# An attention and expert kernel: second pass's first chunk on one batch, two-operand work off GpSimd, the first bias tile in halves

## The chip, the cores and the metric

The kernel runs on one core of one Trainium2 chip. The metric is device time in microseconds, from runs on the chip; one further execution was taken with the hardware profiler. All times below are from these.

## The reference

Three layers follow each other. The first is attention with a bias that a small network computes from the distance of two positions; the second gives every token the weighted sum of four experts; the third multiplies two projections element by element and projects the product.

```python
# B, H, S, D = 2, 8, 576, 64; 1152 tokens of 512; 4 experts of 1024; last layer 1536 wide
scores = q @ k.T / sqrt(D)
x = log1p(abs(i - j)) / log1p(max(i, 1))
scores += (relu(x[..., None] @ w1 + b1) @ w2).transpose(2, 0, 1)
attn = softmax(scores);  x = (attn @ v) as tokens by H * D
p = probs / probs.sum(-1)
x = sum(p[:, e] * (relu(x @ moe_w1[e]) @ moe_w2[e]) for e in range(4))
out = ((x @ w_a) * (x @ w_b)) @ w_out
```

## The kernel before

**A planner writes the program.** Every piece of work is an `op` with the engines that may do it and an estimated cost on each, the tiles it reads and writes, and a rank. `Plan.run` goes through estimated time and gives each free engine the waiting piece of lowest rank that can start; the order so found is each engine's program. On the chip the engines then work through their programs in order and wait for each other by semaphores. A cost, an engine list or a dependency that changes therefore reorders everything behind it. `ENGINES` says which engines may do which kind of piece, `RELUS` how many of a bias group's four lookups ScalarE does. Pools of tiles are `Room`s: a piece starts only when there is a free place for its result, and places are handed out in the order of asking.

**Attention.** The bias is made in 36 groups of 16 rows (`bias_group`): four lookups `hh`, each a maximum against a shifted table on VectorE (L365) or a relu on ScalarE (L367), then four products on TensorE (`pb`, L379), an output `bst` (ScalarE L397 or VectorE L399), a mirror copy of its other side (L236, the shared helper for copies), and a store to DRAM (`bias_d`, L410). A bias tile `bt` for 128 rows and two heads is read back with shifted rows (L466). The first eight groups (rank `bias0`) serve the first 128 rows.

For each pair of heads `m` and batch `b`, rows 0 to 127 come first, then rows 128 to 575 in two parts. Scores `ps` (L516 in plain float32 for the first rows, later L498 with the queries split in a high part `qh` and a rest `ql`, L451), the sum with the bias and the row minimum in one VectorE instruction (L501), the exponential on ScalarE (L511), transposes to `ptb` (L533), one over the row sums (L573, L574, tiles `sums`, `rx`, `rb`), the product with the values `pv` (L598), and the result in two parts, `x_hi` and `x_lo` (L607).

**Experts.** All products are of split operands, high times high, high times low and low times high. A weight unit is loaded to a staging tile `wst` (L639), cast to `wh` (L640) and the rest `wl` is taken (L641). `w1_item` makes the up-products `up` (L730) of one chunk of tokens, one expert and a quarter of its width, and the hidden tile `hh`, `hl` (L757, L758); `w2_item` makes the down-products `pz` (L741) and adds them to `acc`. The tokens are ordered so that the first 128 of both batches are columns 0 to 255, then come 448 of batch 0, then 448 of batch 1. Pass 0 takes chunk 0 (columns 0 to 255) and needs the first attention rows only, so it runs as filler, at a late rank, beside the rest of the attention. Pass 1 takes, for each expert, chunk 1 (columns 256 to 639) and chunk 2 (columns 640 to 1151).

Beside pass 1 the last layer's weights, which come as float64, are taken apart in words on VectorE (`convert`, L658 to L679); for `w_out` one subtraction (L678) may run on GpSimd. Behind the passes a Strassen-like product (`ab_item`, L864) and the last projection follow.

**Places.** Split weights have two places from the start, one in `mid`, one more when the values are done, three in `late` when the bias is done (`bias_end`) and one when attention is done (`attn_end`). The hidden tiles of pass 1 (`h2`) get two places when attention is done.

Of the kernel before, what the change touches and what calls it, by code (L numbers as in the profile page):

```python
# [9 lines left out]
F32 = mybir.dt.float32  # L10
# [9 lines left out]
P = 128  # L20
# [18 lines left out]


RANK = {"prep": 0.5, "bias0": 0, "bias1": 0.6, "bias2": 1, "split": 1, "load": 2, "chain": 0, "fill": 2, "x64": 3, "evac": -0.5, "fin": 0, "pv": 0, "split2": 1.5, "px": 0, "evac2": -0.5, "h2": 0}
ENGINES = {"kcast": "ACT DVE", "ksub": "POOL DVE", "qcast": "DVE", "qsub": "POOL DVE", "pt": "ACT DVE", "tail": "ACT DVE", "side": "ACT DVE", "mirror": "POOL ACT",
           "whi": "ACT DVE", "wlo": "DVE", "xhi": "DVE", "xlo": "POOL DVE", "rb": "ACT DVE", "rx": "ACT DVE", "s64": "POOL DVE",
           "wsum": "POOL DVE", "whi2": "ACT", "wlo2": "DVE", "px": "ACT DVE", "xsum": "DVE", "xhi2": "ACT", "xlo2": "DVE", "hmul": "DVE", "hlo": "DVE"}
QUICK, BY_AGE, MARGIN, LEAD = 0.9, True, 300, 2

# [44 lines left out]
class Plan:  # L91
# [9 lines left out]
    def op(self, eng, fn, r=(), w=(), rw=(), hold=(), prio=0, lock=False, after=(), size=0):  # L101

        o = Op()
        o.eng, o.fn, o.prio, o.lock, o.size = eng, fn, prio, lock, size
        o.after, o.n, o.done = [], len(self.ops), False
        deps = set(after)
        for b in r:
            deps.update(b.writers)
        for b in rw:
            deps.update(b.writers)  # L110
            deps.update(b.readers)
        for b in rw:
# [12 lines left out]
        self.ops.append(o)
        return o
# [102 lines left out]
def tile_kernel(ctx, tc, qd, kd, kf, vd, cst, probs, w1r, w2r, war, wbr, wor, out):  # L229
# [21 lines left out]
    def tp(stack, name, **kw):  # L251
        return stack.enter_context(tc.tile_pool(name=name, bufs=1, reuse_waits="tile", **kw))

    def place(room, pool, tag, n, shape, dt=F32, mark=None, pair=False):
        for i in range(n):
            def make(name, i=i):
                if pair:
                    return tuple(pool.tile(shape, dt, tag=f"{tag}{i}{z}", name=f"{name}{z}", bufs=1) for z in "hl")
                return pool.tile(shape, dt, tag=f"{tag}{i}", name=name, bufs=1)
            room.add(make, 1, mark)  # L260
# [13 lines left out]
    hp = tp(hp_stack, "hp", side="right")  # L274


    R = {z: Room() for z in "w wst h1 h2 u z p q2 q k2 k kq v bt ptb pr rb xf sums rx hh bst ct sum s64 t64 hl64".split()}
    R["s"], R["tv"] = Room(False), Room(False)
    ps_a = tp(attn, "ps_a", space=PSUM)
    ps_b = tp(solo, "ps_b", space=PSUM, side="right")  # L280
# [39 lines left out]
    NG = S // 4  # L320
    cs_t = hp.tile([P, S + NG + NU + 2 + 32], F32, name="cs")
    cs, pos = Buf(t=cs_t), hp.tile([P, NU, max(RELUS.values())], F32, name="pos")
    corr = {n: hp.tile([P, 1], F32, name=f"corr{n}") for n in sorted(set(RELUS.values()))}
    tab, neg_ = cs_t[:, 0:S], cs_t[:, S:S + NG]
    rinv, cw, w2s = cs_t[:, S + NG:S + NG + NU], cs_t[:, S + NG + NU:S + NG + NU + 2], cs_t[:, S + NG + NU + 2:]
    op({"SP": 440}, lambda e: nc.sync.dma_start(out=cs_t, in_=cst), w=[cs], size=P * 3160)
# [27 lines left out]
    rows, early = [], []  # L354

    def bias_group(u, rank):
        pri, acts = RANK[rank], RELUS[rank]
        before, after, n = dist(u)
        hs = []
        for g in range(4):  # L360
            G = 4 * u + g
            hh = new("hh")
            hs.append(hh)
            if g < 4 - acts:
                op({"DVE": n / 1.92 + 130}, lambda e, hh=hh, G=G: nc.vector.tensor_scalar(out=hh.t[:, :n], in0=tab[:, :n], scalar1=neg_[:, G:G + 1], scalar2=None, op0=ALU.max), r=[cs], w=[hh], prio=pri, lock=True)  # L365
            else:
                op({"ACT": n / 1.2 + 220}, lambda e, hh=hh, G=G: nc.scalar.activation(out=hh.t[:, :n], in_=tab[:, :n], func=AF.Relu, bias=pos[:, u, g - 4:][:, :1]), r=[cs], w=[hh], prio=pri)  # L367
        pb = new("tv" if n <= 512 else "s", "pb")
        bst = new("bst")


        def base():
            return (pb.t, 0) if n <= 512 else (pb.t.rearrange("p a b -> p (a b)"), 512 - n // 2)

        def mm(e):
            t, o = base()
            for lo, hi in ((0, n),) if n <= 512 else ((0, n // 2), (n // 2, n)):
                for g in range(4):
                    nc.tensor.matmul(t[32 * g:32 * g + 32, o + lo:o + hi], w2s, hs[g].t[:, lo:hi], start=True, stop=True)  # L379

        op({"PE": n * 1.67 + 170}, mm, r=[*hs, cs], w=[pb], hold=[bst], prio=pri)


        def ends():
            t, o = base()
            b = bst.t
            if before >= after:
                side = b[:, 0:before + 1], t[:, o:o + 1 + before][:, ::-1]
                rest = b[:, before + 1:before + after], b[:, before - after + 1:before][:, ::-1]
            else:  # L390
                side = b[:, before:before + after], t[:, o:o + after]
                rest = b[:, 0:before], b[:, before + 1:2 * before + 1][:, ::-1]
            return side, rest

        def put(e, out, src):
            if e == "ACT":
                nc.scalar.activation(out=out, in_=src, func=AF.Identity, scale=rinv[:, u:u + 1], bias=corr[acts])  # L397
            else:
                nc.vector.tensor_scalar(out=out, in0=src, scalar1=rinv[:, u:u + 1], scalar2=corr[acts], op0=ALU.mult, op1=ALU.add)  # L399

        def mirror(e):
            copy(e, *ends()[1])

        m = min(before, after - 1)
        side = op({e: v + 95 for e, v in t_psum(n, ENGINES["side"]).items()}, lambda e: put(e, *ends()[0]), r=[pb, cr], w=[bst], prio=pri)
        op({e: v for e, v in {"POOL": 2 * m + 150, "ACT": m / 1.2 + 95, "DVE": m / 0.96 + 68}.items() if e in ENGINES["mirror"].split()}, mirror, w=[bst], after=[side], prio=pri)
        rows.append(Buf(t=bias_d))

        def store(e):
            nc.sync.dma_start(out=bias_d[16 * u:16 * u + 16, :, S - before:S + after].rearrange("i h j -> (i h) j"), in_=bst.t[:, :before + after])  # L410

        o = op({"SP": 440}, store, r=[bst], w=[rows[u]], prio=pri, size=P * 4 * (before + after))
        if u == P // 16 - 1:
            early.append(o)
# [41 lines left out]
    def bias_tile(m, t):  # L456
        for x in bias_seq[-3:]:
            if x[:2] == (m, t):
                return x[2]
        bt = new("bt")  # L460
        bias_seq.append((m, t, bt))

        def load(e):
            b = bt.t
            if t < 4:
                nc.sync.dma_start(out=b, in_=bias_rows(t * P, P, 2 * m, 2))  # L466
            else:
                nc.sync.dma_start(out=b[0:D, 0:1], in_=bias_rows(4 * P, D, 2 * m, 1))
                rest = bias_rows(4 * P, D, 2 * m + 1, 1)
                nc.sync.dma_start(out=b[D:P, 0:1, :S - D], in_=rest[:, :, D:])  # L470
                nc.sync.dma_start(out=b[D:P, 0:1, S - D:], in_=rest[:, :, :D])

        need = min(P * t + P, S) // 16
        op({"SP": 440 if t < 4 else 1320}, load, r=rows[:need], w=[bt], size=P * 8 * S)
        return bt

    def step(m, b, t, k, q0, Q, qw, K, ptb, sums):
# [233 lines left out]
    late = {}  # L711
# [34 lines left out]
    def w1_item(p, e, c, q):  # L746
        t0, nt = CHUNKS[c]
        n = nt * P
        h = new("h1" if p == 0 else "h2", "h")
        if (p, e, q, 0) not in WU:  # L750
            WU[p, e, q, 0] = unit(w1r[e, q])
        xs = [X[b, p] for b in range(B)]
        for ft in range(2):
            u, last = up(WU[p, e, q, 0], ft, t0 * P, n, xs, [h])
            for t in range(t0, t0 + nt):
                ups.setdefault(t, []).append(last)
            relu = op({"ACT": n / 1.2 + 68}, lambda en, ft=ft, u=u: nc.scalar.activation(out=h.t[0][:, ft, :n], in_=u.t[:, :n], func=AF.Relu), r=[u], w=[h])  # L757
            op({"DVE": n / 0.96 + 68}, lambda en, ft=ft, u=u: nc.vector.scalar_tensor_tensor(out=h.t[1][:, ft, :n], in0=u.t[:, :n], scalar=0.0, in1=f(h.t[0][:, ft, :n]), op0=ALU.max, op1=ALU.subtract), r=[u], w=[h], after=[relu])  # L758
        return h
# [300 lines left out]

    def bias_end():
        hp_stack.close()
        place(R["w"], tp(ctx, "late", side="right"), "wl", 3, [P, 1024], F32R, pair=True)

    def attn_end():
        attn.close()
# [100 lines left out]
```

## Time and profile before

| | us |
|---|---|
| median of 3 runs | 828.71 (827.18 to 829.26) |
| profiled execution, its own time | 830.67 |
| its span, first to last instruction | 828.9 |
| TensorE busy | 802.6 |
| VectorE busy | 606.4 |
| ScalarE busy | 346.2 |
| GpSimd busy | 62.0 |

In the profile PE is TensorE's matmuls and PEld its weight loads, DVE is VectorE, ACT is ScalarE, POOL is GpSimd and SP the queue that issues nearly all DMAs. A busy matmul is not a matmul at full speed, as they are pipelined and their ends are modelled. A row of a timeline has the start in the span, the time, the engine, the line, the operation, the tiles (out<-in), shapes and count, and in brackets the idle time of the engine before it with the work that ended it. The granted clock of TensorE is a share of 2.4 GHz.

### The profile page before, as it was taken

How to read it: one execution, taken by the hardware profiler on the slowest of the kernel's cores; microseconds unless marked ns; L12 is line 12 of the kernel's file. 1: busy time of each engine (PE TensorE's matmuls, PEld its weight loads, DVE VectorE, ACT ScalarE, POOL GpSimd, SP SyncE). 2: the span in 40 equal slices, each digit the busy share in tenths (PEclk: the TensorE clock that was granted, in tenths of full speed). 3: DMA queues.
4: the chain of work that ended last, by engine and by line, in shares of the span. 5: the costliest groups of instructions: out<-in, count | busy, mean ns of one | idle time of the engine just before them, and what ended most of it. 6: DMA issues, size and time to landing. Idle time of an engine off the chain costs nothing.

```text
span 828.9 us, 12951 instructions
## 1 busy us (share of the span) xinstructions
PE 802.6 (97%) x4939; PEld 671.0 (81%) x4939; DVE 606.4 (73%) x1234; ACT 346.2 (42%) x703; POOL 62.0 (7%) x66
## 2 busy tenths in 40 slices
PE   6999999999989899999999999999999999999997
PEld 2576677888878798887888988888889999899996
DVE  6889886989788568786879897924666565757545
ACT  7877865676757511221122122303345432323211
POOL 1100000121021000000100110000010000000000
PEclk9999999999999999999999999999999999999999
DMA  6987867776554245553556647510303120211103
GB/s 209 342 302 215 286 192 247 251 228 215 181 183 145 68 153 177 191 191 115 164 186 195 197 133 229 174 56 0 102 1 95 59 77 26 77 33 45 51 1 115
DMA packets 49166, 122.39 MB, mean 148 GB/s; under 512 B 5200, under 2 KB 11600, under 8 KB 49104
## 3 DMA queue, kind: packets, MB, share of 16 engines
q1 hardware_dynamic: 48960, 121.44, 45.7%
q8 instruction: 39, 0.64, 0.3%
q14 instruction: 23, 0.19, 0.1%
q10 hardware_dynamic: 144, 0.13, 0.0%
HBM read 95.71 MB, written 25.84 MB: 147 GB/s over the span
## 4 chain that ended last, share of the span: by engine, by line
PE 71%; DVE 14%; DMA 9%; ACT 3%; issue 2%; SPq 0%; DVEq 0%; ACTq 0%
PE pz L741 25%; PE up L730 15%; PE pw L864 9%; PE pr L864 4%; PE pv L598 4%; PE ps L498 3%; PE pt L533 3%; DMA s<-in_wbr 3%; DVE wl L641 2%; PE pq L864 2%; PE pb L379 2%; DMA s<-in_war 2%; DVE pr L501 1%; DMA wst<-in_w2r 1%; DVE hl L758 1%
## 5 line engine op out<-in xcount | busy, mean ns | idle before, releaser
L741 PE MATMUL pz<-wh,hl 128*128 128x512 f32 x386 | 152.8, 396 | 3.2 <-DVE hl L758 3.2
L741 PE MATMUL pz<-wh,hh 128*128 128x512 f32 x386 | 154.8, 401 | 0.0
L741 PE MATMUL pz<-wl,hh 128*128 128x512 f32 x386 | 152.8, 396 | 0.0
L730 PE MATMUL up<-x_hi,wh 128*128 128x256 f32 (+2 forms) x384 | 134.0, 349 | 2.9 <-DVE hl L758 2.8
L730 PE MATMUL up<-x_lo,wh 128*128 128x256 f32 (+2 forms) x384 | 129.9, 338 | 0.1
L730 PE MATMUL up<-x_hi,wl 128*128 128x256 f32 (+2 forms) x384 | 129.8, 338 | 0.0
L757 ACT ACTIVATE hh<-up 128x256 fp32r<-128x256 f32 (+2 forms) x96 | 46.6, 490 | 136.3 <-PE up L730 136.1
L236 ACT CAST wh<-wst 128x1024 fp32r<-128x1024 f32 (+1 forms) x65 | 65.5, 1007 | 81.5 <-PE pz L741 53.9
L741 PEld LDWEIGHTS pz<-wh,hl 128*128 128x128 f32 x386 | 73.0, 189 | 20.1 <-DVE hl L758 5.6
L741 PEld LDWEIGHTS pz<-wh,hh 128*128 128x128 f32 x386 | 72.9, 189 | 17.5 <-issue 3.1
L741 PEld LDWEIGHTS pz<-wl,hh 128*128 128x128 f32 x386 | 72.7, 188 | 17.1
L730 PEld LDWEIGHTS up<-x_hi,wh 128*128 128x128 f32 x384 | 72.4, 188 | 15.4 <-issue 4.8
L641 DVE TENSOR_TENSOR wl<-wst,wh 128x1024 fp32r<-128x1024 f32 x64 | 77.9, 1218 | 9.3 <-ACT wh L236 9.2
L730 PEld LDWEIGHTS up<-x_lo,wh 128*128 128x128 f32 x384 | 72.4, 189 | 6.7 <-DVE x_lo L607 0.3
L730 PEld LDWEIGHTS up<-x_hi,wl 128*128 128x128 f32 x384 | 72.3, 188 | 5.9
L758 DVE SCALAR_TENSOR_TENSOR hl<-up,hh 128x256 fp32r<-128x256 f32 (+2 forms) x96 | 52.1, 551 | 25.9 <-ACT hh L757 25.3
L501 DVE CUSTOM_DVE_ANT_0 pr<-ps,bt 128x576 f32<-128x576 f32 (+1 forms) x80 | 59.7, 751 | 13.2 <-PE ps L498 10.9
L236 ACT COPY ct<-pw 128x512 f32<-128x512 f32 (+3 forms) x48 | 27.8, 579 | 97.9 <-PE pw L864 97.8
L511 ACT ACTIVATE pr<-pr,sums 128x576 f32<-128x576 f32 x72 | 55.9, 777 | 18.4 <-DVE sums L501 15.4
L236 ACT COPY ptb<-pt 128x512 f32<-128x512 f32 (+3 forms) x88 | 37.4, 451 | 24.6 <-PE pt L533 21.5
L598 PE MATMUL pv<-ptb,v 128*64 128x128 f32 (+2 forms) x480 | 44.1, 331 | 1.2 <-ACT ptb L236 0.6
L365 DVE TENSOR_SCALAR hh<-cs 128x576 f32<-128x576 f32 (+17 forms) x108 | 42.1, 447 | 3.3 <-PE pb L379 3.1
(159 smaller groups left out, 1416.8 us busy)
## 6 DMA issues: line engine op xcount, KB each, us to landing
wst<-in_w1r SPq DMA_DIRECT2D x32, 512.0 KB, 4.2
wst<-in_w2r SPq DMA_DIRECT2D x32, 512.0 KB, 4.9
bias_d<-bst SPq DMA_DIRECT2D x36, 295.5 KB, 3.3
bt<-bias_d SPq DMA_DIRECT2D x16, 576.0 KB, 5.3
v<-in_vd SPq DMA_DIRECT2D x24, 320.0 KB, 4.7
s<-in_war SPq DMA_DIRECT2D x12, 512.0 KB, 5.3
wz_d<-hl SPq DMA_DIRECT2D x24, 256.0 KB, 2.8
s<-in_wbr SPq DMA_DIRECT2D x12, 512.0 KB, 5.2
```

What stands on the lines that cost most here:

```text
L236: (nc.scalar.copy if e == "ACT" else engine[e].tensor_copy)(out, in_)
L365: op({"DVE": n / 1.92 + 130}, lambda e, hh=hh, G=G: nc.vector.tensor_scalar(out=hh.t[:, :n], in0=tab[:, :n], scalar1=neg_[:, G:G + 1], sca ...
L498: nc.tensor.matmul(ps.t[:, half, o:o + w], lhs, K.t[:, s, k0:k0 + w], start=(kk == 0 and n < 2), stop=(kk == 1 and n in (0, len(runs) - 1)))
L501: nc.vector.tensor_tensor_reduce(out=pr.t[r0:r1, c].rearrange("p (a b) -> p a b", a=2), in0=ps.t[r0:r1, :, :HS], in1=bt.t[r0:r1, c].rearra ...
L511: nc.scalar.activation(out=pr.t[:, c], in_=pr.t[:, c], func=AF.Exp, scale=-1.0, bias=sums.t[:, neg:neg + 1], accum_out=sums.t[:, col:col + 1])
L598: nc.tensor.matmul(pv.t[s * D:(s + 1) * D, :w], V.t[:, s, kt * D:(kt + 1) * D], ptb.t[:, blk, :w], start=(kt == 0), stop=(kt == 4))
L641: op(t_two(1024, ENGINES["wlo"]), lambda e: engine[e].tensor_tensor(out=w.t[1], in0=wst.t, in1=f(w.t[0]), op=ALU.subtract), r=[wst], rw=[w ...
L730: nc.tensor.matmul(u.t[:, :n], a[:, d, ft * P:(ft + 1) * P], x[:, d, lo:lo + n], start=(d == 0 and j == 0), stop=(d == 3 and j == 2))
L741: nc.tensor.matmul(z.t, a[:, ft, tt * P:(tt + 1) * P], bb[:, ft, :], start=(first and ft == 0 and j == 0), stop=(final and ft == 1 and j = ...
L757: relu = op({"ACT": n / 1.2 + 68}, lambda en, ft=ft, u=u: nc.scalar.activation(out=h.t[0][:, ft, :n], in_=u.t[:, :n], func=AF.Relu), r=[u] ...
L758: op({"DVE": n / 0.96 + 68}, lambda en, ft=ft, u=u: nc.vector.scalar_tensor_tensor(out=h.t[1][:, ft, :n], in0=u.t[:, :n], scalar=0.0, in1= ...
L864: nc.tensor.matmul(o_, s[:, k], d[:, k], start=(first and k == 0 and i == 0), stop=(k == 1 and i == 2), skip_group_check=True)
```

## The change

Five edits. The lists of `ENGINES` lose GpSimd for the rest of the queries (`qsub`) and for the float64 subtraction (`s64`), and the mirror copies of the first eight bias groups (`mirror0`) go to ScalarE or VectorE. In every odd one of these eight groups VectorE does all four lookups; `corr` is then made for the counts 0 and 1. The first bias tile is loaded in two halves, each dependent on its own four stores. Chunk 1 of pass 1 depends on batch 0's tokens alone, and its hidden tiles come from a room of their own, `h3`, of two places that open with the end of the bias; `late` gets two places for split weights instead of three.

```diff
-ENGINES = {..., "qsub": "POOL DVE", ..., "mirror": "POOL ACT",
+ENGINES = {..., "qsub": "DVE", ..., "mirror": "POOL ACT", "mirror0": "ACT DVE",
-           ..., "s64": "POOL DVE",
+           ..., "s64": "DVE",
...
-    corr = {n: hp.tile([P, 1], F32, name=f"corr{n}") for n in sorted(set(RELUS.values()))}
+    corr = {n: hp.tile([P, 1], F32, name=f"corr{n}") for n in range(max(RELUS.values()) + 1)}
...
     def bias_group(u, rank):
-        pri, acts = RANK[rank], RELUS[rank]
+        pri, acts = RANK[rank], RELUS[rank] if u % 2 == 0 or rank != "bias0" else 0
...
         need = min(P * t + P, S) // 16
-        op({"SP": 440 if t < 4 else 1320}, load, r=rows[:need], w=[bt], size=P * 8 * S)
+        if t == m == 0:
+            for h in range(2):
+                r = slice(D * h, D * h + D)
+                op({"SP": 440}, lambda e, h=h, r=r: nc.sync.dma_start(out=bt.t[r], in_=bias_rows(D * h, D, 0, 2)), r=rows[4 * h:4 * h + 4], w=[bt], size=D * 8 * S)
+        else:
+            op({"SP": 440 if t < 4 else 1320}, load, r=rows[:need], w=[bt], size=P * 8 * S)
...
     def w1_item(p, e, c, q):
-        h = new("h1" if p == 0 else "h2", "h")
+        h = new(("h1", "h3", "h2")[c], "h")
...
-        xs = [X[b, p] for b in range(B)]
+        xs = [X[b, p] for b in range(B if c != 1 else 1)]
...
     def bias_end():
-        place(R["w"], tp(ctx, "late", side="right"), "wl", 3, [P, 1024], F32R, pair=True)
+        place(R["w"], tp(ctx, "late", side="right"), "wl", 2, [P, 1024], F32R, pair=True)
+        place(R["h3"], tp(ctx, "late3", side="right"), "h", 2, [P, 2, 3 * P], F32R, pair=True)
```

The order of the instructions changes nearly everywhere up to the last product. The lines of the new kernel are 5 higher behind the bias load (L741 becomes L746).

On SP, at the first bias tile, the order before is this; `bst` with its number is one group's output, the numbers rise with the group, and `bt` is the bias tile:

```order
L410 DMA bias_d_92<-bst_230 128x591
L410 DMA bias_d_92<-bst_252 128x591
L410 DMA bias_d_92<-bst_264 128x591
L410 DMA bias_d_92<-bst_282 128x591
L410 DMA bias_d_92<-bst_303 128x591
L466 DMA bt_341<-bias_d_92 128x2x576
L619 DMA v_348<-in_vd 128x640
L619 DMA v_353<-in_vd 128x640
```

In the new order, at the same place:

```order
L410 DMA bias_d_92<-bst_235 128x591
L477 DMA bt_274<-bias_d_92 64x2x576
L410 DMA bias_d_92<-bst_252 128x591
L410 DMA bias_d_92<-bst_269 128x591
L410 DMA bias_d_92<-bst_286 128x591
L410 DMA bias_d_92<-bst_307 128x591
L477 DMA bt_274<-bias_d_92 64x2x576
L624 DMA v_351<-in_vd 128x640
```

The first half of the tile stands four stores earlier, the second half where the whole tile stood.

On GpSimd, from the middle of attention into pass 1, the order before has the query rests `ql` and the float64 words `s` among the x_lo:

```order
L607 TENSOR_TENSOR x_lo<-xf,x_hi 128x192
L607 TENSOR_TENSOR x_lo<-xf,x_hi 128x256
L451 TENSOR_TENSOR ql<-q_3020,qh 128x512
...
L451 TENSOR_TENSOR ql<-q_3149,qh 128x512
...
L451 TENSOR_TENSOR ql<-q_3301,qh 128x384
L451 TENSOR_TENSOR ql<-q_3419,qh 128x384
...
L678 TENSOR_TENSOR s_4015<-s_4015,hl_4053 128x512
L678 TENSOR_TENSOR s_4384<-s_4384,hl_4434 128x512
```

In the new order VectorE has the float64 subtraction (L683) between its other words and the hidden tiles of pass 1:

```order
L763 SCALAR_TENSOR_TENSOR hl<-up,hh 128x384
L683 TENSOR_TENSOR s_3994<-s_3994,hl_4032 128x512
...
L667 TENSOR_SCALAR t_4059<-t_4059 128x512
L668 SCALAR_TENSOR_TENSOR s_4023<-s_4023,t_4059 128x512
L763 SCALAR_TENSOR_TENSOR hl<-up,hh 128x512
L684 TENSOR_TENSOR hl_4032<-s_3994 128x512
L671 TENSOR_SCALAR t_4059<-s_4023 128x512
L672 SCALAR_TENSOR_TENSOR s_4023<-s_4023,t_4059 128x512
L683 TENSOR_TENSOR s_4023<-s_4023,hl_4060 128x512
```

Nine `ql` and ten `s` subtractions of GpSimd are VectorE's now, and three x_lo of the first rows; nine later x_lo, thirteen mirror copies of the later bias groups and ten sums of the last layer stay on GpSimd.

On TensorE, at the end of attention, the order before has no expert work between the last scores and the last value product (`pv`):

```order
L550 MATMUL pt<-ident,pr 128x128
L598 MATMUL pv<-ptb,v 64x192 x10
L533 MATMUL pt<-ident,pr 128x128 x4
L552 MATMUL pt<-ident,pr 128x128
L553 MATMUL pt<-ident,pr 64x128
L578 MATMUL rp<-ident,rx 128x128
L580 MATMUL rp<-ident,sums 128x128
L598 MATMUL pv<-ptb,v 64x192 x10
L730 MATMUL up<-x_hi,wh 128x384
```

In the new order:

```order
L746 MATMUL pz<-wl,hh 128x512
L603 MATMUL pv<-ptb,v 64x192 x10
L538 MATMUL pt<-ident,pr 128x128 x4
L746 MATMUL pz<-wh,hh 128x512
...
L557 MATMUL pt<-ident,pr 128x128
L558 MATMUL pt<-ident,pr 64x128
L583 MATMUL rp<-ident,rx 128x128
L585 MATMUL rp<-ident,sums 128x128
L735 MATMUL up<-x_hi,wh 128x384
...
L603 MATMUL pv<-ptb,v 64x192 x10
```

Two groups of six down-products of pass 0 stand around the last value product but one, and twelve up-products of chunk 1 stand ahead of the last one.

## Rows read from the trace of the kernel before

**Rows 1.** The page, busy us, share of span and instructions of each engine.

```profile
PE 802.6 (97%) x4939; PEld 671.0 (81%) x4939; DVE 606.4 (73%) x1234; ACT 346.2 (42%) x703; POOL 62.0 (7%) x66
```

**Rows 2.** Stretches: length, busy PE, PEld, DVE, ACT, POOL, clock, DMA share, GB/s.

```profile
27.66:62.38 34.72, 33.18 (x330) 24.32 (x328) 31.96 (x100) 26.41 (x67) 2.54 (x5) 1.00 0.94 333
...
62.00:271.00 209.00, 202.00 (x1514) 162.67 (x1513) 177.74 (x389) 142.13 (x307) 26.57 (x26) 1.00 0.67 215
271.00:288.00 17.00, 14.73 (x123) 11.07 (x121) 9.44 (x27) 9.61 (x26) 0.73 (x1) 1.00 0.19 54
288.00:605.00 317.00, 313.78 (x1441) 264.55 (x1440) 232.98 (x406) 72.45 (x115) 16.69 (x10) 0.99 0.47 148
```

**Rows 3.** First bias tile: timeline (start, us, work, [idle before]), chain, DMA issues.

```profile
18.56 0.76 DVE L399 TENSOR_SCALAR bst<-pb,cs,corr 128x464 f32<-128x464 f32 x1 [1.46 <-PE pb L379]
...
23.07 4.57 DMA bt<-bias_d
...
27.66 0.76 DVE L501 CUSTOM_DVE_ANT_0 pr<-ps,bt 128x576 f32<-128x576 f32 x1 [1.26 <-DMA bt<-bias_d]
...
28.34 0.75 DVE L501 CUSTOM_DVE_ANT_0 pr<-ps,bt 128x576 f32<-128x576 f32 x1
...
bias_d<-bst SPq DMA_DIRECT2D x36, 295.5 KB, 3.3
```

**Rows 4.** VectorE groups, 27 to 62.4 us (busy, mean ns); then TensorE.

```profile
L236 DVE COPY ptb<-pt 128x512 f32<-128x512 f32 x7 | 4.5, 682 | 0.0
...
L573 DVE TENSOR_SCALAR sums<-sums 128x2 f32<-128x2 f32 x8 | 1.5, 186 | 0.0
L607 DVE TENSOR_TENSOR x_lo<-xf,x_hi 128x128 fp32r<-128x128 f32 x5 | 1.4, 286 | 0.1
...
L641 DVE TENSOR_TENSOR wl<-wst,wh 128x1024 fp32r<-128x1024 f32 x1 | 1.2, 1214 | 0.0
...
L365 DVE TENSOR_SCALAR hh<-cs 128x304 f32<-128x304 f32 x1 | 0.4, 366 | 0.0
...
65.97 0.39 PE L730 MATMUL up<-x_hi,wh 128*128 128x256 f32 x1 [0.76 <-DVE hl L758]
...
68.67 0.72 PE L379 MATMUL pb<-hh,cs 128*32 128x304 f32 x8
```

**Rows 5.** Query subtractions: a VectorE group, then the timeline.

```profile
L451 DVE TENSOR_TENSOR ql<-q,qh 128x512 fp32r<-128x512 f32 x4 | 2.7, 676 | 0.0
...
193.32 0.54 PE L498 MATMUL ps<-k,qh 128*128 128x288 f32 x2 [0.48 <-DVE sums L501]
...
233.20 1.94 POOL L451 TENSOR_TENSOR ql<-q,qh 128x512 fp32r<-128x512 f32 x1 [11.47 <-PE ps L498]
234.03 1.14 DVE L573 TENSOR_SCALAR sums<-sums 128x3 f32<-128x3 f32 x1
...
236.56 0.53 PE L498 MATMUL ps<-k,qh 128*128 128x288 f32 x2 [1.23 <-DVE sums L501]
...
248.71 0.53 PE L498 MATMUL ps<-k,qh 128*128 128x288 f32 x2 [0.24 <-DVE sums L501]
```

**Rows 6.** Second pass: timeline near 376 us, a stretch, chain pieces.

```profile
370.85 0.42 DVE L662 TENSOR_SCALAR t<-t 128x512 uint32<-128x512 uint32 x1
...
375.51 1.75 POOL L678 TENSOR_TENSOR s<-s,hl 128x512 f32<-128x512 f32 x1 [49.57 <-ACT hh L757]
...
376.03 1.52 DVE L662 TENSOR_SCALAR t<-t 128x512 uint32<-128x512 uint32 x1
...
378.80 0.50 PE L741 MATMUL pz<-wh,hl 128*128 128x512 f32 x1 [1.95 <-DVE hl L758]
...
379.74:383.15 3.41, 3.41 (x10) 2.62 (x9) 2.16 (x4) 0.00 (x0) 0.00 (x0) 0.50 0.26 97
...
315.14 4.92 PE pz L741 x20
...
378.80 6.47 PE pz L741 x20
```

More of the change, by code (lines that the diff above doesn't have):

```diff
@@ L41 @@
 RANK = {"prep": 0.5, "bias0": 0, "bias1": 0.6, "bias2": 1, "split": 1, "load": 2, "chain": 0, "fill": 2, "x64": 3, "evac": -0.5, "fin": 0, "pv": 0, "split2": 1.5, "px": 0, "evac2": -0.5, "h2": 0}
-ENGINES = {"kcast": "ACT DVE", "ksub": "POOL DVE", "qcast": "DVE", "qsub": "POOL DVE", "pt": "ACT DVE", "tail": "ACT DVE", "side": "ACT DVE", "mirror": "POOL ACT",
-           "whi": "ACT DVE", "wlo": "DVE", "xhi": "DVE", "xlo": "POOL DVE", "rb": "ACT DVE", "rx": "ACT DVE", "s64": "POOL DVE",
+ENGINES = {"kcast": "ACT DVE", "ksub": "POOL DVE", "qcast": "DVE", "qsub": "DVE", "pt": "ACT DVE", "tail": "ACT DVE", "side": "ACT DVE", "mirror": "POOL ACT", "mirror0": "ACT DVE",
+           "whi": "ACT DVE", "wlo": "DVE", "xhi": "DVE", "xlo": "POOL DVE", "rb": "ACT DVE", "rx": "ACT DVE", "s64": "DVE",
            "wsum": "POOL DVE", "whi2": "ACT", "wlo2": "DVE", "px": "ACT DVE", "xsum": "DVE", "xhi2": "ACT", "xlo2": "DVE", "hmul": "DVE", "hlo": "DVE"}
@@ L274, in tile_kernel @@
     hp = tp(hp_stack, "hp", side="right")
-    R = {z: Room() for z in "w wst h1 h2 u z p q2 q k2 k kq v bt ptb pr rb xf sums rx hh bst ct sum s64 t64 hl64".split()}
+    R = {z: Room() for z in "w wst h1 h2 h3 u z p q2 q k2 k kq v bt ptb pr rb xf sums rx hh bst ct sum s64 t64 hl64".split()}
     R["s"], R["tv"] = Room(False), Room(False)
@@ L405, in bias_group @@
         side = op({e: v + 95 for e, v in t_psum(n, ENGINES["side"]).items()}, lambda e: put(e, *ends()[0]), r=[pb, cr], w=[bst], prio=pri)
-        op({e: v for e, v in {"POOL": 2 * m + 150, "ACT": m / 1.2 + 95, "DVE": m / 0.96 + 68}.items() if e in ENGINES["mirror"].split()}, mirror, w=[bst], after=[side], prio=pri)
+        op({e: v for e, v in {"POOL": 2 * m + 150, "ACT": m / 1.2 + 95, "DVE": m / 0.96 + 68}.items() if e in ENGINES["mirror0" if rank == "bias0" else "mirror"].split()}, mirror, w=[bst], after=[side], prio=pri)
         rows.append(Buf(t=bias_d))
```

## The prediction

> **What bounds the kernel now.** I read the page first: TensorE is busy 97% of the span, no other engine over 73% [rows 1]. So time can only go where TensorE waits. The busy times by stretch say where that is [rows 2]. From 62 to 271 us (attention with expert work as filler) it idles 7.0 us, and VectorE is busy 177.74 of 209 us, 85%. From 271 to 288 us (attention with no filler left) it idles 2.27 us, and from 288 to 605 us (experts, second pass) 3.2 us. From 27.66 us, the first use of a bias tile, to 62.38 us, the last x_lo of the first 128 tokens, there is no filler, and TensorE (33.18) and VectorE (31.96 of 34.72 us) are both near their limit. Behind 605 us, in the last product, the order of TensorE is the same in both kernels, so I look no further there.
>
> Then I read who ended the waits, in the timelines. First, a TENSOR_SCALAR of VectorE that takes 0.19 us on average at the start took 1.14 us while GpSimd ran a two-operand subtraction beside it, and TensorE's next matmul waited 1.23 us for VectorE [rows 4, 5]. Second, the same at 376 us: an instruction that had taken 0.42 us took 1.52 us, TensorE waited 1.95 us, and behind the wait a granted clock of 0.50, the 1.2 GHz level, stands for 3.41 us [rows 6]. Twenty down-matmuls from 378.80 took 6.47 us, where twenty at full clock took 4.92 us: 1.55 us more.
>
> **The start (first 62 us).** The parts: every odd one of the first eight bias groups takes all four table lookups on VectorE, their mirror copies go from GpSimd to ScalarE, and the first bias tile comes in two halves. ScalarE loses four lookups. VectorE gains four of about 0.4 us, 1.6 us, and it idled 1.46 us before one output of such a group [rows 3], so most of it fits in. I take 0.7 us for the last of the eight groups (bounds 0 and 1.46). The first half of the tile needs four early stores; on SP it stands between stores that wait for their own data, so I cost it at nothing. The second half has 288 KB instead of 576. The whole tile took 4.57 us to land; a store of 295.5 KB takes 3.3 us [rows 3]. Bounds 0 and 1.27, I take 1.2, as the store is nearer in size. So the first use of the tile, now at 27.66 us with a wait of 1.26 us in front, comes 1.9 us earlier.
>
> What is late next is VectorE. From the order I count what it does from there to the last x_lo: five lookups more (0.37 us each), three x_lo more that GpSimd did (0.29), one weight split more (1.21 and a cast, taken as long as a ptb copy, 0.68), one bias output more (0.76), three copies of 128 columns more (taken like an x_lo, 0.29), two large ptb copies less (0.68) [rows 3, 4]. That is 1.85 + 0.87 + 1.89 + 0.76 + 0.87 - 1.36 = 4.9 us; neighbours overlap by 0.08 us (27.66 + 0.76 against a start at 28.34 [rows 3]), for twelve instructions 1.0, so 3.9 us. Against it stand 34.72 - 31.96 = 2.8 us of gaps there [rows 2]; I take half of them, 1.4 us, as filled. And the lookups and the split are work that before did just behind the first filler, where TensorE made the bias products of two groups (0.72 us each) and waited 0.76 us for VectorE [rows 4]: products and wait, 2.2 us, come back. Sum: -1.9 + 3.9 - 1.4 - 2.2 = -1.6 us; I take -1.5. Bounds: -3.0 (all gaps filled) and +1.7 (no gap filled, the tile no earlier).
>
> **Subtractions of queries off GpSimd (62 to 271 us).** Nine go to VectorE, at 0.68 us for 512 columns [rows 5], the narrower ones less, 6.1 us at most; the holds that they caused end. Four waits of TensorE stand right behind such holds: 0.48, 1.23, 0.40 and 0.24 us (the first, the longest and the last in [rows 5]). A hold is 1.14 - 0.19 = 0.95 us; the long wait loses that, the others go entirely: 0.48 + 0.95 + 0.40 + 0.24 = 2.1 us. The addition to VectorE lies beside filler matmuls. If that cover is gone, 6.1 us less four holds of 0.95, 2.3 us, come on top. Bounds -2.4 and +2.3; I take -2.1, because the waits are seen and 15% of VectorE is free.
>
> The Trainium skill's page "SBUF — State Buffer", section "Who interferes with whom", states that a VectorE instruction in a two-port mode or with two SBUF inputs and a GpSimd instruction that reads SBUF exclude each other, and that the second one waits for the whole of the other. The held instruction of [rows 5] agrees: both ended together. The rule also speaks against the change: the moved subtractions have two SBUF inputs, so the copies and x_lo that stay on GpSimd can hold them in turn. With one hold of 0.95 us for each of the nine, the term above would be +6.5 instead of -2.1 us; no row shows such a hold, and it counts within the second rival.
>
> **Second pass's first chunk on batch 0 alone.** In the new order the stretch without filler, 2.27 us idle [rows 2], is gone: twelve down-matmuls of the first pass and twelve up-matmuls of the new chunk stand between the last scores and the last value product. I take -2.3 us, bounds -2.3 and 0 (nothing, if the filler kept for the end is missing earlier). All that the new dependency itself adds ahead of the end of attention are those twelve matmuls of 384 columns.
>
> **The float64 words' subtraction off GpSimd (288 to 605 us).** Ten go to VectorE. The hold at 376 us was 1.52 - 0.42 = 1.1 us of the 1.95 us wait; with 0.85 us left I expect no half clock behind it, so 1.1 + 1.55 = 2.65 us go [rows 6]. Bounds -3.5 (the whole wait and the clock) and 0 (another such wait). VectorE gets 10 x 0.68 = 6.8 us in 317 us, of which it is busy 232.98 [rows 2]; TensorE's work hides that. If it doesn't, a wait like the one at 376 us comes back.
>
> **New order and fewer weight places.** The second pass interleaves its two chunks differently, and the places for split weights go from eight to seven. I allow +0.7 us for new waits, bounds 0 and +3.5 (one like that at 376 us with its clock).
>
> **Sum**, against the profiled execution's own 830.67 us (span 828.9 and 1.8 us around it): -1.5 - 2.1 - 2.3 - 2.65 + 0.7 = -7.85 us, 822.8 us. The median of the runs shown, 828.71 us, is 2 us lower; the same difference makes it 820.9 us. About 0.3%, 2.5 us, is what a measurement of this kernel can tell from no change.
>
> **Rivals.**
> More goes. TensorE idles 12.5 us from 62 to 605 us [rows 2]; I remove 2.1 + 2.3 + 1.1 = 5.5 of it. If 10.5 us go, with the 1.55 us of clock, the start's 3.0 and the 0.7 lost, the time is 828.71 - 14.35 = 814.4. For it: nearly all waits have one cause, a late VectorE. Against it: 4.9 us of them are waits of attention behind no hold, and those have no edit.
>
> VectorE takes it back. It gains 6.1 us where it is 85% busy, 6.8 us behind, and 3.9 us at the start. With the start at +1.7, attention at +2.3, the tail at -2.3, the words at -2.65 and +0.7, the time is 828.5: no change. Against it: the gaps of [rows 2]. The Trainium skill's "Perfetto Trace Analysis", section "Optimizing Scalar/DVE Operations", advises to move work off a saturated VectorE to ScalarE or even GpSimd, and warns that VectorE and GpSimd share a port. By its advice this rival wins; by the holds of [rows 5] the warning weighs more.
>
> Slower: the weight places. In the second pass an expert has eight split weights in use when chunk 1 turns into chunk 2; with seven places the last w2 waits until the first w1 has had its last up-matmuls. Its split (0.68 and 1.21 us on VectorE, as above) is covered by 24 up-matmuls of 512 columns, 5.9 us at the 4.92 us that twenty of that width take [rows 6]. It decides from the point where the fetch, too, falls behind the release: 4.57 us, what the nearest load of 576 KB took [rows 3], and 1.9 us are over 5.9 us, and VectorE's queue comes on top. With a wait of 1.95 us and 1.55 us of clock for each of four experts, 14 us, the time is 820.9 + 14 = 834.9. For it: SP's queue is in order. Against it: the fetch goes to a staging tile of its own and can come before.
>
> **How the numbers follow.** Forecast 0.50 (817 to 826), more 0.20 (812 to 817), taken back 0.18 (826 to 830), slower 0.12 (about 835). The range is 812.5 to 829.5. Faster by over 0.3% (below 826.2): the first two and a little of the third, 0.72; within 0.3%: 0.16; slower: 0.12.
>
> **What would show it.** The first bias-tile reduction near 25.8 us; the first up-matmul between 58 and 62 us; no first instruction of the reciprocals over 0.5 us; TensorE idle under 0.7 us in the last 17 us of attention; no half clock between 300 and 605 us. Wrong would be waits of TensorE for VectorE in the second pass of over 2 us in sum, or a half clock there, above all at chunk 2's first down-matmuls.

## The result and the profile after

| us | before | after |
|---|---|---|
| median (runs) | 829.26 (7) | 819.12 (7) |
| lowest and highest | 827.18, 833.82 | 817.95, 824.92 |
| profiled execution, span | 828.9 | 816.2 |
| first up-product | 60.12 | 62.27 |
| TensorE idle to there | 7.75 | 7.72 |
| TensorE idle from there to the last value product | 9.26 | 3.76 |
| TensorE idle in the second pass | 3.22 | 1.31 |
| TensorE idle behind it | 1.76 | 1.77 |

The ratio of after to before is 0.9881, 95% interval 0.9849 to 0.9914: faster, by 10.1 us between the medians. The prediction was 820.9 us, in a range from 812.5 to 829.5. The idle times are sums over the trace; the second pass is counted from the last value product to the first product of the last layer. The two profiled spans differ by 12.7 us, since before's profiled execution (830.67 us) lies above its median and after's (817.95 us) is the quickest of its seven. Two executions far from all others are left out below, with their traces: one of e1 (2737.56 us, the profiled one) and one of the kernel before (977.04 us).

The page of after answers to [rows 1]: busy us, share of the span and instructions of each engine.

```profile
PE 797.4 (98%) x4939; PEld 670.4 (82%) x4939; DVE 618.2 (76%) x1278; ACT 334.9 (41%) x688; POOL 22.2 (3%) x38
```

GpSimd lost 40 of 62 us, and VectorE gained 12. TensorE has as many instructions as before, 5.2 us less busy time and, in 27 waits instead of 43, 7.4 us less idle time. An estimate accounts for most of the 5.2: a wait costs some 0.16 us more than its idle time, as the modelled end of the matmul ahead of it counts as busy (the wait of 1.95 us ahead of 378.80 put 2.11 us more than usual between two starts), which is 2.6 us for 16 waits, and the half clock of [rows 6] made 1.7 us of busy time.

Stretches of after, as in [rows 2] (length, busy PE, PEld, DVE, ACT, POOL with counts, clock, DMA share, GB/s); the second is the last 17 us of attention:

```profile
62.00:271.00 209.00, 205.24 (x1560) 167.26 (x1553) 178.58 (x410) 141.41 (x312) 10.78 (x16) 1.00 0.64 204
265.64:282.64 17.00, 17.00 (x134) 14.13 (x129) 11.78 (x28) 8.75 (x21) 0.73 (x1) 1.00 0.34 86
288.00:605.00 317.00, 315.69 (x1489) 267.50 (x1488) 244.23 (x435) 73.84 (x125) 0.74 (x1) 1.00 0.48 147
```

TensorE idles 3.76 us of the first 209 instead of 7.0, nothing at the end of attention instead of 2.27 of 17, and the clock is full throughout. VectorE is as busy up to 271 us as before (178.58 against 177.74), with nine subtractions more.

The start did not become quicker. The chain of waits of after, near the first bias tile (start, us, piece):

```profile
20.12 4.18 DMA bias_d<-bst
24.29 0.02 SPq L477
...
24.35 3.88 DMA bt<-bias_d
...
28.25 0.76 DVE pr L506
```

A store took 4.18 us to land, the second half of the tile went behind it, and the first use came at 28.25 us. In [rows 3] it came at 27.66.

The view that tells most is who waited for whom. TensorE's waits of before from the first up-product to the last value product (line, waited for, us in total, times, longest):

```profile
PE ps L498 <- DVE sums L501: 3.8, 8, 1.2
PE up L730 <- DVE hl L758: 2.8, 3, 1.9
PE pv L598 <- ACT ptb L236: 0.6, 1, 0.6
PE rp L578 <- DVE ptb L236: 0.6, 1, 0.6
PE pv L598 <- DVE ptb L236: 0.6, 1, 0.6
PE pt L552 <- DVE xf L604: 0.4, 1, 0.4
```

The same of after:

```profile
PE up L735 <- DVE hl L763: 1.9, 2, 1.0
PE pt L538 <- ACT pr L516: 0.7, 1, 0.7
PE rp L583 <- ACT rx L236: 0.6, 1, 0.6
PE pv L603 <- PE pt L538: 0.2, 1, 0.2
```

The scores' waits for VectorE's reductions (`ps` for `sums`, 3.8 us) are gone, and so are the three waits of 0.6 us at the end (the 0.6 us for `rp` that after still has stands at 152.68 us). These two groups are what the experiments follow.

### The profile page after: what moved, and what is told of

Its sections match the earlier page's. It is cut to its first block, busy times and chain, and to the rows that moved or that the text cites. A ratio compares the mean times of both kernels' runs of the same rounds, so it can differ in the third digit from the quotient of the medians.

```text
span 816.2 us, 12864 instructions
## 1 busy us (share of the span) xinstructions
PE 797.4 (98%) x4939; PEld 670.4 (82%) x4939; DVE 618.2 (76%) x1278; ACT 334.9 (41%) x688; POOL 22.2 (3%) x38
## 4 chain that ended last, share of the span: by engine, by line
PE 75%; DVE 12%; DMA 9%; ACT 2%; issue 2%; SPq 0%; DVEq 0%; ACTq 0%
PE pz L746 24%; PE up L735 17%; PE pw L869 10%; PE pv L603 5%; PE pr L869 4%; PE ps L503 4%; PE pt L538 3%; PE pb L379 3%; DMA s<-in_wor 2%; PE pq L869 2%; DMA wst<-in_w1r 2%; DMA s<-in_war 2%; DVE wl L646 2%; DVE hl L763 1%; DVE s L668 1%
## 5 line engine op out<-in xcount | busy, mean ns | idle before, releaser
L746 PE MATMUL pz<-wh,hh 128*128 128x512 f32 x386 | 154.0, 399 | 0.0
L746 PE MATMUL pz<-wl,hh 128*128 128x512 f32 x386 | 152.1, 394 | 0.1
L746 PE MATMUL pz<-wh,hl 128*128 128x512 f32 x386 | 151.7, 393 | 0.0
L735 PE MATMUL up<-x_hi,wh 128*128 128x384 f32 (+2 forms) x384 | 134.2, 349 | 3.2 <-DVE hl L763 3.2
L735 PE MATMUL up<-x_hi,wl 128*128 128x384 f32 (+2 forms) x384 | 129.6, 338 | 0.0
L735 PE MATMUL up<-x_lo,wh 128*128 128x384 f32 (+2 forms) x384 | 129.6, 337 | 0.0
L746 PEld LDWEIGHTS pz<-wl,hh 128*128 128x128 f32 x386 | 72.5, 188 | 17.2 <-DVE wl L646 0.5
L746 PEld LDWEIGHTS pz<-wh,hh 128*128 128x128 f32 x386 | 72.6, 188 | 17.0 <-issue 2.8
L746 PEld LDWEIGHTS pz<-wh,hl 128*128 128x128 f32 x386 | 72.6, 188 | 14.4
L236 ACT CAST wh<-wst 128x1024 fp32r<-128x1024 f32 (+1 forms) x53 | 52.9, 998 | 69.3 <-PE pz L746 60.6
L236 ACT COPY ptb<-pt 128x512 f32<-128x512 f32 (+3 forms) x91 | 39.4, 458 | 20.9 <-PE pt L538 18.4
L538 PE MATMUL pt<-ident,pr 128*128 128x128 f32 x288 | 43.2, 276 | 1.8 <-ACT ptb L236 1.0
L365 DVE TENSOR_SCALAR hh<-cs 128x560 f32<-128x560 f32 (+17 forms) x112 | 43.7, 445 | 1.5 <-PE pb L379 1.1
```

Of the source, the lines that this page charges most:

```text
L236: (nc.scalar.copy if e == "ACT" else engine[e].tensor_copy)(out, in_)
L538: nc.tensor.transpose(pt.t[:, kt * P:kt * P + P], pr.t[:, s, k0:k0 + P], ident)
L735: nc.tensor.matmul(u.t[:, :n], a[:, d, ft * P:(ft + 1) * P], x[:, d, lo:lo + n], start=(d == 0 and j == 0), stop=(d == 3 and j == 2))
L746: nc.tensor.matmul(z.t, a[:, ft, tt * P:(tt + 1) * P], bb[:, ft, :], start=(first and ft == 0 and j == 0), stop=(final and ft == 1 and j = ...
```

## The experiments

The edits were made on the kernel before, singly or in small groups (e1 to e4, e12), and undone in the changed kernel (e5 to e10); e11 varies one of them. The planner makes a new order each time, so no run changes a single wait alone. Medians are given with the ratio to the kernel before on the same chip and its 95% interval; the medians of before were 829.16 (e1 to e4), 829.37 (e5 to e8) and 829.08 us (e9 to e12).

### One part at a time on the kernel before

**e1 and e12: both subtractions off GpSimd.**

```diff
-"qsub": "POOL DVE", ... "s64": "POOL DVE"
+"qsub": "DVE", ... "s64": "DVE"
```

> The kernel before with one edit: the rests of the queries and the float64 subtraction lose GpSimd. Theory 1 (the holds cost what the prediction says): -2.1 in attention and -2.65 us in the second pass, 824.5 us. Theory 2 (more goes; the new profile's second pass is about 5 us shorter at equal work): -2.1 and -5, 822 us. Theory 3 (VectorE takes it back): 828 to 830 us. Under 1 and 2 no reciprocal's first instruction takes over 0.5 us and no half clock stands in the second pass.

> The kernel before with both subtractions off GpSimd, once more for its trace, as the first profiled execution was disturbed. 826.9 us. If the holds' term was right and the tail is untouched: no held reciprocal, waits in attention about 2 us less than before, the waits at the end of attention as before; in the second pass either no wait over 1 us (then -2.65 and only attention falls short), or new waits for VectorE in the place of the one at 376 us.

Measured: 826.65 us, 0.9977 (0.9960 to 0.9994), and again 827.99 us, 0.9977 (0.9955 to 0.9999). In the second pass of e12 the place of [rows 6] reads (timeline: start, us, work, idle before):

```profile
376.60 0.42 DVE L662 TENSOR_SCALAR t<-t 128x512 uint32<-128x512 uint32 x1
377.05 0.69 DVE L663 SCALAR_TENSOR_TENSOR s<-s,t 128x512 uint32<-128x512 uint32 x1
377.66 1.01 DVE L758 SCALAR_TENSOR_TENSOR hl<-up,hh 128x384 fp32r<-128x384 f32 x2
...
378.27 0.51 PE L741 MATMUL pz<-wh,hl 128*128 128x512 f32 x1 [1.00 <-DVE hl L758]
```

The instruction that GpSimd had held for 1.1 us takes its 0.42 us, the wait is 1.00 us instead of 1.95, and the clock stays whole. The second pass takes 314.6 us instead of 317.2: the words' term of the prediction, 2.65 us, stands here to a tenth. Attention does not follow. No reciprocal is held any more, and yet TensorE's waits in it are:

```profile
PE ps L498 <- DVE sums L501: 3.1, 6, 1.2
PE up L730 <- DVE hl L758: 2.8, 3, 1.9
PE pt L533 <- ACT pr L511: 1.4, 1, 1.4
PE rp L578 <- DVE ptb L236: 0.9, 2, 0.7
PE pv L598 <- DVE ptb L236: 0.2, 1, 0.2
```

The last value product starts 0.7 us later than before. Part of that is clock: behind the wait of 1.85 us that ends at 144.81 the granted clock of e12 was 0.50 for 3.41 us, where before's stayed at 1.00 behind 1.86 us at 145.12. But the waits themselves are still there. The holds stood beside the waits of the scores and were not their only cause: without them 3.1 of 3.8 us remain, in a new order, and the longest is 1.24 us (at 233.84) where it was 1.23.

**e2: two late weight places.**

```diff
-        place(R["w"], tp(ctx, "late", side="right"), "wl", 3, [P, 1024], F32R, pair=True)
+        place(R["w"], tp(ctx, "late", side="right"), "wl", 2, [P, 1024], F32R, pair=True)
```

> The kernel before with two late places for split weights instead of three, and nothing else. The prediction's allowance: +0.7 us, 830 us. Its slower rival: a wait of TensorE at each expert's turn to chunk 2, up to +14 us, 843 us. If places cost nothing: 829.3 us with TensorE's waits in the second pass as before, about 3 us in sum.

Measured: 833.97 us, 1.0057 (1.0041 to 1.0073), 4.8 us slower. TensorE waits 4.77 us in the second pass instead of 3.22, in nine waits for hidden tiles instead of three, the longest 1.4 us. That is 1.55 us more, but idle time alone understates what waits cost. An estimate from the starts of the matmuls, summed as far as their distance exceeds the usual one (0.232 us for 512 columns, 0.174 for 384), gives 9.8 us lost in the second pass of e2 and 7.5 in that of before, 1.7 of them by the half clock. Without the clock that is 4.0 us, where the medians differ by 4.8. The slower rival's direction exists; its 14 us don't.

**e3: chunk 1 on batch 0, own hidden tiles, two late places.** The edit of e2, `xs` of chunk 1 on one batch, and the room `h3`, as in the diff of the change.

> The kernel before with chunk 1 on batch 0 alone, its own two hidden tiles and two late places for split weights; GpSimd and the start as before. Theory 1 (only the tail of attention gains): -2.3 + 0.7, 827.7 us, with the wait at 376 us or one like it still there. Theory 2 (the own hidden tiles also let the second pass run without waits, and this is where the unforeseen 2 us of it come from): -2.3 - 2.5, 824.5 us.

Measured: 826.41 us, 0.9974 (0.9956 to 0.9992). Against e2 that is 7.6 us: the edit of the chunk pays for the place and 2.8 us more. But not at the tail. TensorE's three waits of 0.65, 0.59 and 0.61 us at the end of attention are all there, ahead of the twelve up-products; these were only moved. What fell are the waits of the second pass, 1.98 us instead of 3.22 (4.77 in e2).

**e4: the three edits of the start.**

```diff
+... RELUS[rank] if u % 2 == 0 or rank != "bias0" else 0
+"mirror0": "ACT DVE"
+        if t == m == 0:   # two loads of 64 rows, each behind its own four stores
```

> The kernel before with the three edits of the start: odd early groups without ScalarE's lookups, their mirror copies off GpSimd, the first bias tile in halves. The prediction: -1.5 us, 827.8 us. Theory 2, from the new profile (the first half holds back the two last stores on SP, so the tile is complete at 28.2 instead of 27.6 us, and the first up-product starts 2.2 us later): between 0 and +2 us, 829 to 831 us, tile complete near 28.2 us here too.

Measured: 828.01 us, 0.9989 (0.9972 to 1.0007): no change that can be told. First use of the tile at 27.81 us, first up-product at 62.42.

### One part taken back from the changed kernel

**e5: the tile loaded whole.** The branch `if t == m == 0` is taken out.

> The changed kernel with the first bias tile loaded whole, as before. By the prediction (the halves bring 1.9 us earlier use): 821 us, 2 us over the changed kernel. Theory 2 (the first half blocks SP for two stores, so the halves cost 0.6 us): 818.5 us, the first reduction at 27.3 us or earlier instead of 28.25.

Measured: 820.70 us, 0.9906 (0.9883 to 0.9928), which overlaps the changed kernel's interval. First use at 26.89 us. In the chain of e5 the load of the tile goes right behind the issue of the tenth store, the last one ahead of it in SP's order; the eight that it needs have landed by then:

```profile
21.57 0.32 SPq L410
...
22.12 4.75 DMA bt<-bias_d
26.89 0.76 DVE pr L501
```

e10 has the halves; its eighth store was issued at the same time as e5's (18.60 and 18.66 us). Its chain:

```profile
18.60 4.33 DMA bias_d<-bst
22.93 0.02 SPq L477
...
22.99 3.92 DMA bt<-bias_d
26.93 0.76 DVE pr L506
```

The store that in e5 landed after 2.9 us (at 21.57) takes 4.33 us here, while the first half of the tile is under way (issued at 17.00, landed at 21.26). In the seven kernels with halves the eighth store takes 3.65 to 4.62 us, in the six without 2.57 to 2.95. The second half is 0.83 us quicker than the whole tile and starts 0.87 us later. The five other kernels with halves on SP (after, e4, e7, e8, e9) first use the tile at 26.75 to 28.25 us, the five others without (before, e2, e3, e6, e12) at 27.23 to 27.66.

In after the half also blocked SP. It waited for the fourth store, which took 4.26 us (2.66 in e10) and landed at 18.64, and was issued at 18.79; stores 7 and 8, whose data were there at 18.34 and 19.21, went behind it at 19.52 and 20.12. Why the fourth store, ahead of any half, takes 4.07 to 4.45 us in six of the traces and 2.64 to 2.70 in the other seven, with and without halves, stays open. So a part of after's 28.25 us is not the halves' doing.

**e11: the first half on ScalarE's queue.**

```diff
-op({"SP": 440}, lambda e, h=h, r=r: nc.sync.dma_start(...))
+op({("ACT", "SP")[h]: 440}, lambda e, h=h, r=r: (nc.scalar, nc.sync)[h].dma_start(...))
```

> The changed kernel with the first half of the first bias tile issued by ScalarE's queue, so that SP's stores 7 and 8 don't stand behind it. If the block on SP is what ate the halves' gain: first reduction at 26.5 us or earlier and the time 818 us or less. If the DMA engines' sharing of the traffic is: first reduction near 27.4 us, 819 us. ScalarE may wait for the fourth store: then its lookups are late, and 820 us.

Measured: 821.46 us, 0.9906 (0.9879 to 0.9933), first use at 27.93 us. With the half off SP's queue the eighth store, issued at 19.00, still needs 3.65 us, as the first half is under way until 20.84; two more stores then put the second half to 23.91. So the store is slow beside the half's traffic, whichever queue issues the half. The order of the second pass came out worse here, with 5.80 us of waits; more on it below.

**e6: no edit of the start.**

> The changed kernel without the three edits of the start. The five edits one by one and in pairs brought 1.9, 2.1 and 0.9 us, 5 us together, but the whole change 9.9. If the start adds only its own 0.9 us: 820 us. If it is what the other edits need: 823 to 824 us.

Measured: 822.86 us, 0.9928 (0.9907 to 0.9949): 3.7 us over the changed kernel, with intervals that just touch. Attention idles 5.39 us instead of 3.76, 2.76 of it in one wait at 145 us for a hidden tile, where the changed kernel has none; behind it the granted clock was 0.50 for 3.41 us in this execution. The e5 kernel, which has the lookups and mirror copies of the change, has a wait of 1.58 us there; the kernels with halves have at most 0.7 us between 140 and 155 us. Their bias ends earlier in the order (last bias product at 126 to 130 us instead of 132 to 133). What the halves are worth may lie there; with 1.6 us between the medians of e5 and of the changed kernel it isn't shown.

**e7: chunk 1 on both batches again**, hidden tiles from the places of chunk 2, still two late weight places.

> The changed kernel with chunk 1 dependent on both batches and its hidden tiles in the places of chunk 2, still two late weight places. If the parts add up: the 2.1 us of the chunk's edit and the 4.7 us that the lost weight place costs without it, 826 us, with the waits in the second pass. If the chunk's edit is worth only its tail: 821.4 us.

Measured: 827.89 us, 0.9985 (0.9967 to 1.0004), 8.8 us over the changed kernel. Attention is as good as there (3.71 us idle, nothing waits for `sums`); the second pass idles 5.78 us instead of 1.31. One of its waits, VectorE and TensorE:

```profile
285.53 0.43 DVE L663 TENSOR_SCALAR t<-s 128x512 uint32<-128x512 uint32 x1 [4.02 <-DMA s<-in_war]
...
288.32 1.01 DVE L763 SCALAR_TENSOR_TENSOR hl<-up,hh 128x384 fp32r<-128x384 f32 x2
...
288.93 0.50 PE L746 MATMUL pz<-wh,hl 128*128 128x512 f32 x1 [1.06 <-DVE hl L763]
```

VectorE stood 4.02 us at a float64 load that had not landed, the hidden tiles were queued behind it, and TensorE had nothing left. Estimated by starts, as for e2, the second pass loses 11.4 us here and 2.4 in after, 9.0 us more, about what the medians differ by. The prediction's rival had weights in mind; every one of the ten waits is for a hidden tile. Not all of these stand behind float64 work: ahead of the longest wait, 1.41 us at 598.43, VectorE is idle and makes the tile as soon as ScalarE's part is there, so the order has no other work at that place. Whether the missing weight place keeps it away wasn't separated.

**e8, e9 and e10: both subtractions, the queries alone, the words alone may go to GpSimd again.** Edits: the entries of `ENGINES` as before.

> The changed kernel with both subtractions allowed on GpSimd again. If the parts add up: 1.9 us, 821 us. If the missing 5 us of the whole lie in the holds (with own hidden tiles a hold of VectorE is late at once): 824 us, with holds of 0.7 to 1.1 us and a wait of TensorE behind each in the second pass.

> The changed kernel with only the queries' rests allowed on GpSimd again; the order then has no down-products of pass 0 around the last value products but one, as with both subtractions back. Theory 1 (the tail's cover and the holds in attention are both the queries' doing): waits of 0.6 us at the end of attention return, three of them, and holds of 0.7 to 1.1 us; +2.1 + 1.9, 823 us. Theory 2 (the tail is chunk 1's doing, as the prediction had it): +2.1 us, 821.2 us, no waits at the end.

> The changed kernel with only the float64 subtraction allowed on GpSimd again; the order up to the end of attention stays. Prediction's term: +2.65 us, 821.8 us, with a wait of over 1 us in the second pass. If the own hidden tiles of chunk 1 give VectorE enough lead: +0 to +0.9 us, 819 to 820 us, and waits under 1 us although holds are there.

Measured: 824.96 us, 0.9951 (0.9932 to 0.9970); 824.60 us, 0.9952 (0.9933 to 0.9970); 819.83 us, 0.9900 (0.9874 to 0.9926). The queries are worth 5.5 us and the words 0.7, of which only the first is clear of noise. TensorE's waits in attention of e9:

```profile
PE ps L503 <- DVE sums L506: 3.8, 8, 1.1
...
PE pv L603 <- ACT ptb L236: 0.6, 1, 0.6
PE rp L583 <- DVE ptb L236: 0.6, 1, 0.6
PE pv L603 <- DVE ptb L236: 0.6, 1, 0.6
...
```

Both groups of before are back, together. In the words' case, e10, holds are there and cost little (timeline, GpSimd and VectorE):

```profile
391.22 1.76 POOL L683 TENSOR_TENSOR s<-s,hl 128x512 f32<-128x512 f32 x1 [37.02 <-DVE t L671]
391.73 1.54 DVE L667 TENSOR_SCALAR t<-t 128x512 uint32<-128x512 uint32 x1
```

GpSimd did six such subtractions in e10 and held VectorE for 0.6 to 1.1 us in each, and no wait of TensorE stands behind this one. The second pass idles 3.03 us instead of 1.31, and its longest wait is 1.45 us.

### What the thirteen kernels have in common

The scores' waits for `sums` come to 3.0 to 3.8 us in seven kernels and to 0 to 1.6 us in six (after, e5, e6, e7, e10, e11). The six share two things, queries off GpSimd and two late weight places. Each of the seven lacks one at least: before and e4 both, e2, e3, e8 and e9 the first, e12 the second. The tail goes with them: in the six at most one wait of over 0.3 us is left there, of 0.41 us in e5 and e6 and of 0.82 us in e7. No run has the pair alone. In the order that the planner makes for it, the last six down-products of pass 0 stand between the last value products, as in the six (in after behind the last but one, in e5 between the last but two and the last but one). In the seven all of them stand ahead of the last three value products. So by the order the filler that covers attention's end comes from the pair; what the pair alone is worth was not measured. Which of the moved instructions ends the waits in the middle of attention wasn't separated.

No kernel tried is faster than the changed one: e10, e5 and e11 are within its interval.

## Why the prediction was right, and where its steps were not

The time was right (819.12 us against 820.9), the sign and the size too, but in part by luck: of the five terms only the words' came out as argued, and only on the kernel before, and the errors of the others nearly cancelled. Step by step:

- **What bounds it: right.** Nearly all that was gained was TensorE waiting for late work of VectorE (one wait of 0.65 us was for ScalarE), in the stretches named, and the clock behind one such wait. Behind 605 us nothing changed (idle 1.76 and 1.77 us).
- **The start, -1.5 us: the step on the first half failed.** "On SP it stands between stores that wait for their own data, so I cost it at nothing." Its 288 KB were in the way of the eighth store, 4.33 us instead of 2.9 (e10 and e5), and in after it held stores 7 and 8 back on SP by 1.2 and 0.9 us. The second half landed in 3.88 us instead of 4.57, 0.7 us where 1.2 was taken. The first use was forecast near 25.8 us and came at 28.25; the first up-product came at 62.27, just past the bounds of 58 to 62. Alone the edits gave 1.2 us, not clear of noise; in company 3.7, with intervals that touch.
- **The queries, -2.1 us: right in sign, wrong in its mechanism.** The step that failed is that four waits go because the holds behind them end. In e12 the holds are gone and 3.1 of 3.8 us of the scores' waits stay, with one as long as the 1.23 us that was to lose 0.95. With two late places the same edit removes all 3.8 us, of which 2.1 were counted. VectorE did take the work without loss, at 0.676 us for 512 columns as in [rows 5] (groups of VectorE in after, 62 to 271 us):

```profile
L451 DVE TENSOR_TENSOR ql<-q,qh 128x512 fp32r<-128x512 f32 x6 | 4.1, 676 | 0.0
L578 DVE TENSOR_SCALAR sums<-sums 128x4 f32<-128x4 f32 x8 | 1.3, 165 | 0.0
L578 DVE TENSOR_SCALAR sums<-sums 128x3 f32<-128x3 f32 x7 | 1.1, 163 | 0.8 <-ACT pr L516 0.8
```

- **The tail, -2.3 us: right in size, put down to the wrong edit.** In e3 the chunk's edit is there and the waits stay; in e7 it is gone and the down-products cover the tail, but for one wait of 0.82 us. By the order it belongs to the queries with the two places. The order showed what stands there; it does not tell which edit put it there, and the prediction read it as if it did.
- **The words, -2.65 us: right alone, 0.7 in company.** e12's trace gives 2.6 us in the second pass. The 1.55 us of clock in this term belong to the profiled execution of before: the clock does not fall in every one (see the last section). In the changed kernel the same holds are mostly covered, so this gain overlaps with that of the chunk's edit.
- **The chunk and the places, +0.7 us: wrong.** The lost place costs 4.8 us alone (e2), and the chunk's edit with it brings 7.6 to 8.8 us. The prediction gave the chunk only its tail. In the second pass TensorE's waits are 1.31 us in sum, below the 2 us named as the limit.
- **What comes next** is neither weights nor a held instruction. The one longer wait of the second pass of after:

```profile
458.18 0.43 DVE L663 TENSOR_SCALAR t<-s 128x512 uint32<-128x512 uint32 x1 [4.66 <-DMA s<-in_war]
...
459.56 0.69 DVE L668 SCALAR_TENSOR_TENSOR s<-s,t 128x512 uint32<-128x512 uint32 x1
460.18 0.55 DVE L763 SCALAR_TENSOR_TENSOR hl<-up,hh 128x384 fp32r<-128x384 f32 x1
...
460.78 0.50 PE L735 MATMUL up<-x_hi,wh 128*128 128x512 f32 x1 [0.97 <-DVE hl L763]
```

A float64 load lands late, and VectorE waits 4.66 us for it, with the hidden tile four instructions behind. In e11 the same place has 5.00 us, and a wait of TensorE of 3.16.

**The rivals.** "More goes" had 10.5 us of idle time going; 7.4 went. "VectorE takes it back" did not happen, although VectorE is busier. The Trainium skill's page "SBUF — State Buffer", section "Who interferes with whom", counted for it that the moved subtractions can be held by what stays on GpSimd. In after no row shows VectorE held in attention. The hold falls on the other side: a mirror copy of 79 columns took 1.60 us, where one of 111 took 0.48, and VectorE's split `wl`, with two operands, ran beside it in its usual 1.22 us:

```profile
118.88 1.60 POOL L236 COPY bst<-bst 128x79 f32<-128x79 f32 x1 [17.49 <-DVE hh L365]
119.14 1.22 DVE L646 TENSOR_TENSOR wl<-wst,wh 128x1024 fp32r<-128x1024 f32 x1
```

The copy ended 0.12 us behind the split. That agrees with the rule as the prediction gave it, one of the two waiting for the other, and no wait of TensorE in after is put down to GpSimd. The slower rival is the part that the whole change hides: e2 and e7 show its sign, at 4.8 and 8.8 us, by another mechanism than the one argued.

So the sum came out by errors of both signs. Undone one at a time in the changed kernel, the edits are worth 5.5 (queries), 0.7 (words), 3.7 (start) and 8.8 us (chunk), less 4.8 for the place (from e2, as no run gives the changed kernel its third place back), 13.9 together; alone they gave 1.1 and 2.5 (both subtractions, twice), 2.8 (chunk and places) and 1.2 us (start). The whole is 10.1 by medians. No set of single terms can add up to that.

## What to carry to other kernels

Where a planner makes the order, a wait that stands behind a slow instruction isn't yet caused by it: look whether the wait has filler in front of it, and ask which edit keeps filler for that place. Splitting a load brought nothing here, as its early part ran beside the very stores that the late part waits for. When several edits are made at once, undo each one in the whole: alone, the lost weight place cost 4.8 us and the words gained 2.6; in company the place was paid back, and the words' 0.7 us can't be told from nothing.

## What the hardware showed that was not expected

The length of a wait alone does not decide whether the clock falls. Behind 1.95 us (before, at 378.80) the granted clock was 0.50, the 1.2 GHz level, for 3.41 us, and behind 2.71 us in e4 it fell as well:

```profile
383.00:385.00 2.00, 2.00 (x6) 1.52 (x5) 1.06 (x2) 0.00 (x0) 0.00 (x0) 0.50 0.28 105
```

In e11 TensorE waited 3.16 us up to 465.14, and the clock stayed whole:

```profile
465.00:467.00 2.00, 1.86 (x8) 1.59 (x9) 1.93 (x6) 0.00 (x0) 0.00 (x0) 1.00 0.00 0
```

TensorE had no idle time in the 20 us ahead of any of these three waits. The same place of the program shows both, too: in attention the clock stayed at 1.00 behind 1.86 us (before, at 145.12) and was 0.50 for 3.41 us behind 1.85 (e12, at 144.81), 1.94 (e3) and 2.76 us (e6). What tells them apart stays open.

It also differs between executions of one program. Of 73 executions of before that were measured beside the experiments, 23 had a mean granted clock of 0.999 or 1.000 and a median of 827.2 us, twelve one of 0.995 or 0.996 and a median of 831.8. In after, six of seven had 1.000 (median 818.8 us), and the seventh, 0.997, took 824.92. So, as an estimate across chips, some 8 of the 10 us are gained where the clock is whole in both kernels, and the rest goes with a clock that falls in fewer executions.

And e4's profiled execution had a granted clock of 0.95 outside the stretch at 0.50, which is neither of the two levels, and its span was 829.4 us, near before's 828.9.
